# The gate's small working tiles placed in the buffer of the token sums

## Chip, cores, metric

One core of a Trainium2 chip runs the whole program. The metric is the device time of one execution in microseconds (us), smaller being better.

## The reference

Attention with a multiplicative decay, and behind it a mixture of experts in which every expert sees every token and the gate weighs them after eight rounds of normalising over experts and over tokens:

```python
scores = scale * np.matmul(q, k.transpose(0, 1, 3, 2))        # 4 batches, 8 heads, 576 x 64
scores = np.where(causal, -1e9, scores + decay)
attn = softmax(scores); x = (attn @ v) as [2304, 512]

logits = x @ w_gate                                            # 8 experts
P = np.exp(logits - logits.max())
for _ in range(8):
    P /= P.sum(1, keepdims=True) + 1e-09
    P /= P.sum(0, keepdims=True) + 1e-09
    P *= N / E
for e in range(E):
    out += P[:, e:e + 1] * (np.maximum(x @ w1[e], 0.0) @ w2[e])
```

## The kernel before, in words

The attention runs first and leaves x transposed in on-chip memory as two parts, `x_hi` and `x_lo`; every product is made of three matmuls of such parts. Then come the experts. Their work is a list `work` of items (pass n, expert e, quarter fb of the hidden width); a pass takes 768 of the 2304 tokens. In this document "item 0" is the first of that list. Items 0 to 7 alternate experts 1 and 0 and are plain; from item 8 on the first product is the fast form (`first_fast`, seven half-size products, L1032), which needs sums of blocks of x (`T_HI`, `T_LO`) and of w1 (`wsum`).

For each item the program writes, in this order:

- loads of the next item's w1 halves and of this item's w2 halves, all on SP's one queue, in order (L693);
- the first product (`first_plain`, PE L702), with its relu and remainder on ACT (`hh`, L708) and DVE (`hl`, L711);
- the split of the next item's w1 (ACT cast L978, then the remainder on DVE L979; for fast items the sums on POOL, L985 to L999);
- the second product of the item **before** (`second`, PE L722, six 128-token tiles or two, six matmuls each), added into `acc` on DVE;
- the split of this item's w2, in two halves: ACT cast L978, POOL remainder L979. There is one w2 buffer, so these run between one second product and the next. The raw w2 half is free for the next load when L979 has read it.
- in some items, `token_sums(g, c)`: eight POOL operations into the tile `ts` (L958 to L965), an ACT cast of all of it into `T_HI` (L966), and a POOL subtraction for `T_LO` (L967). `ts` has one buffer. In pass 0 they are written after items 3 and 5. A third group, for the next pass, is written later and its POOL operations are brought forward.

The gate's eight rounds (`gate_weights`) are a generator that is advanced a step at a time between matmul groups of items 0 to 4. A round is nine small DVE operations on `prob` and small tiles `rs`, `cs`, `ca`, and one PE matmul with a matrix of ones (`pc`, L941), which waits for DVE's `cs` (L936). The last operation of a round is L945 on DVE.

The order in each engine's queue around this part is made by the recording layer's scheduler: it places an instruction once its inputs and its buffer are there by its own reckoning, so operations may stand well ahead of where the program writes them. At run time each engine goes through its queue in order.

Of the kernel before, what the change touches and what calls it, by code (L numbers as in the profile page):

```python
# [8 lines left out]
F32 = mybir.dt.float32  # L9
# [5 lines left out]
P = 128  # L15
# [117 lines left out]
def attention_then_moe(  # L133
# [14 lines left out]
    E, _, F = w1.shape  # L148
# [6 lines left out]
    NTILE = N // P  # L155
# [707 lines left out]
    HT = N // 6  # L863
# [5 lines left out]
    acc_p = ctx.enter_context(tc.tile_pool(name="acc", bufs=1))  # L869
    tp = ctx.enter_context(tc.tile_pool(name="tp", bufs=1))  # L870
    up = ctx.enter_context(tc.tile_pool(name="up", bufs=1))
    gp = ctx.enter_context(tc.tile_pool(name="gp", bufs=1))
    acc += [acc_p.tile([P, DM], F32, name=f"acc{t}") for t in range(AHEAD // P, PT)]
    acc_1 = [acc_p.tile([P, DM], F32, name=f"acc1_{t}") for t in range(PT)]

# [26 lines left out]

    def gate_weights():

        lg = gp.tile([P, NTILE, E], F32, name="lg")
        pl = psum.tile([P, NTILE, E], F32, tag=GATE, name="pl")

        for a in range(0, N, DM):
            w = min(DM, N - a)
            nc.sync.dma_start(out=acc_1[a // DM][0:E, 0:w], in_=lg_d[:, a:a + w])  # L910
        for _ in range(4):
            yield
        for t in range(NTILE):
            a, o = divmod(t * P, DM)
            nc.tensor.transpose(pl[:, t, :], acc_1[a][0:E, o:o + P], ident[0:E, 0:E])
        nc.vector.tensor_copy(lg, pl)
        mx = gp.tile([P, 1], F32, name="mx")
        nc.vector.tensor_reduce(out=mx, in_=lg.rearrange("p t e -> p (t e)"), axis=AX.X, op=ALU.max)
        yield

        pm = psum.tile([P, P], F32, tag=GATE, name="pm")
        nc.tensor.transpose(pm, mx.to_broadcast([P, P]), ident)
        ma = gp.tile([P, 1], F32, name="ma")
        nc.vector.tensor_reduce(out=ma, in_=pm, axis=AX.X, op=ALU.max)
        nc.vector.tensor_scalar_mul(ma, ma, -1.0)
        nc.scalar.activation(out=prob, in_=lg, func=AF.Exp, bias=ma)
        for _ in range(8):
            rs = gp.tile([P, NTILE], F32, tag="rs", name="rs")
            nc.vector.tensor_reduce(out=rs, in_=prob, axis=AX.X, op=ALU.add)
            nc.vector.tensor_scalar_add(rs, rs, 1.0e-9)  # L930
            nc.vector.reciprocal(rs, rs)
            nc.vector.tensor_tensor(
                out=prob, in0=prob, in1=rs.unsqueeze(2).to_broadcast([P, NTILE, E]), op=ALU.mult
            )
            cs = gp.tile([P, E], F32, tag="cs", name="cs")
            nc.vector.tensor_reduce(out=cs, in_=prob.rearrange("p t e -> p e t"), axis=AX.X, op=ALU.add)  # L936
            for _ in range(3):
                yield
            ca = gp.tile([P, E], F32, tag="ca", name="ca")
            pc = psum.tile([P, E], F32, tag=GATE, name="pc")  # L940
            nc.tensor.matmul(pc, ones, cs, start=True, stop=True)  # L941
            nc.vector.tensor_scalar_add(ca, pc, 1.0e-9)
            nc.vector.reciprocal(ca, ca)
            nc.vector.tensor_scalar_mul(ca, ca, float(N) / E)
            nc.vector.tensor_tensor(  # L945
                out=prob, in0=prob, in1=ca.unsqueeze(1).to_broadcast([P, NTILE, E]), op=ALU.mult
            )
# [166 lines left out]
    for m, (n, e, fb, segs, fast) in enumerate(work):  # L1114
        if m + 1 < len(work):
            r1 = raw("w1", *work[m + 1][1:3])
        r2 = raw("w2", e, fb)
        if m == 0:
            pending.append(gate_weights())
            go_on()  # L1120
        hts = hts_of[m % 2]
        tags = EARLIER if m < PLAIN_0 else FIRST
        if fast:
            first_fast(segs[0][0], hts, tags)
        else:
            first_plain(segs, hts, tags)
        if n > 0 and m in sums_at:
            token_sums(*sums_at[m])
        if m + 1 < len(work):
            if work[m + 1][4]:  # L1130
                split_sums(r1, weight_sums(r1))
            else:
                split_whole("w1", r1, nc.vector)
        if late:
            if late[:3] == (0, 1, GATED):
                while pending:
                    go_on()
            second(*late)
        split_whole("w2", r2, nc.vector if n > 0 and not fast else nc.gpsimd)
        if n == 0 and m in sums_at:  # L1140
            token_sums(*sums_at[m])
        late = (n, e, fb, segs, hts)
# [27 lines left out]
```

## Time and profile before

| | |
|---|---|
| median of 3 runs | 1770.77 us (1770.63 to 1771.16) |
| the profiled execution's own time | 1770.57 us |
| its span, first to last instruction | 1768.8 us |
| granted TensorE clock, mean | 0.996 of full |
| PE busy | 1725.3 us |
| DVE busy | 1344.6 us |
| POOL busy | 1134.9 us |
| ACT busy | 682.8 us |

PE is the tensor engine, PEld its weight loads, DVE the vector, ACT the scalar and POOL the GpSimd engine, SP the one that issues transfers. The time is the span and 1.8 us around it. A busy PE counts a matmul to its modelled end, so what PE loses is read from its waits and from its clock. The gate's rounds lie between 288 and 338 us of the span, and the first fast item begins at 377 us.

### The profile page before, as it was taken

How to read it: one execution, taken by the hardware profiler on the slowest of the kernel's cores; microseconds unless marked ns; L12 is line 12 of the kernel's file. 1: busy time of each engine (PE TensorE's matmuls, PEld its weight loads, DVE VectorE, ACT ScalarE, POOL GpSimd, SP SyncE). 2: the span in 40 equal slices, each digit the busy share in tenths (PEclk: the TensorE clock that was granted, in tenths of full speed). 3: DMA queues.
4: the chain of work that ended last, by engine and by line, in shares of the span. 5: the costliest groups of instructions: out<-in, count | busy, mean ns of one | idle time of the engine just before them, and what ended most of it. 6: DMA issues, size and time to landing. Idle time of an engine off the chain costs nothing.

```text
span 1768.8 us, 26556 instructions
## 1 busy us (share of the span) xinstructions
PE 1725.3 (98%) x9355; PEld 1521.6 (86%) x9355; DVE 1344.6 (76%) x2278; ACT 682.8 (39%) x1456; POOL 1134.9 (64%) x1067
## 2 busy tenths in 40 slices
PE   7999998999999999989999999999999999999998
PEld 5777776788999999879999999999899999999997
DVE  6887785967778777757778777777577877777786
ACT  6766662333333333233333333333333333333332
POOL 6675746366766666666766666676566666667662
PEclk9999999999999999999999999999999999999999
DMA  6433331222222222132212222222311222222221
GB/s 162 127 101 107 104 88 32 90 90 72 61 66 72 72 66 72 54 102 72 64 62 72 72 66 72 72 60 66 107 60 60 72 72 66 72 72 61 65 72 60
DMA packets 146596, 135.20 MB, mean 76 GB/s; under 512 B 65176, under 2 KB 116384, under 8 KB 146464
## 3 DMA queue, kind: packets, MB, share of 16 engines
q1 hardware_dynamic: 146464, 133.52, 24.9%
q8 instruction: 73, 1.20, 0.3%
q14 instruction: 59, 0.48, 0.1%
HBM read 128.61 MB, written 4.87 MB: 75 GB/s over the span
## 4 chain that ended last, share of the span: by engine, by line
PE 73%; POOL 2%; issue 1%; ACT 0%; DVE 0%; DMA 0%; POOLq 0%
PE po L722 39%; PE ph L1032 33%; PE ph L702 1%; POOL t L967 1%; POOL early_w L979 0%; POOL ts L958 0%; ACT t L966 0%; POOL ts L959 0%; DMA w<-in_moe_w_dram 0%; DVE hl L711 0%; POOL ts L964 0%; POOL ts L963 0%; POOL ts L961 0%; POOL ts L965 0%; POOL ts L960 0%
## 5 line engine op out<-in xcount | busy, mean ns | idle before, releaser
L722 PE MATMUL po<-early_w,hh 128*128 128x512 f32 x2304 | 719.7, 393 | 10.9 <-POOL early_w L979 9.2
L722 PEld LDWEIGHTS po<-early_w,hh 128*128 128x128 f32 x2304 | 430.5, 189 | 101.3 <-POOL early_w L979 12.8
L1038 DVE TENSOR_TENSOR u<-ph,u 128x384 f32<-128x384 f32 x588 | 319.9, 556 | 193.9 <-PE ph L1032 188.0
L1083 DVE SCALAR_TENSOR_TENSOR acc<-po,prob,acc 128x512 f32<-128x512 f32 x532 | 381.2, 742 | 102.3 <-PE po L722 102.3
L722 PE MATMUL po<-early_w,hl 128*128 128x512 f32 x1152 | 452.1, 392 | 0.0
L998 POOL TENSOR_TENSOR early_w<-ws,early_w 128x1024 fp32r<-128x1024 f32 x84 | 202.2, 2408 | 280.3 <-ACT early_w L995 280.3
L711 DVE SCALAR_TENSOR_TENSOR hl<-u,hh 128x384 fp32r<-128x384 f32 x336 | 376.6, 1121 | 1.8 <-ACT hh L708 1.7
L978 ACT CAST early_w<-w 128x512 fp32r<-128x512 f32 x216 | 133.7, 622 | 560.7 <-POOL ws L985 442.3
L708 ACT ACTIVATE hh<-u 128x384 fp32r<-128x384 f32 x336 | 175.4, 523 | 297.4 <-DVE u L1038 297.4
L1032 PE MATMUL ph<-t,early_w 128*128 128x384 f32 x1512 | 275.6, 334 | 0.0
L979 POOL TENSOR_TENSOR early_w<-w,early_w 128x512 fp32r<-128x512 f32 x184 | 235.3, 1299 | 59.0 <-ACT early_w L978 59.0
L1032 PEld LDWEIGHTS ph<-t,early_w 128*128 128x128 f32 x1512 | 264.0, 188 | 0.0
L722 PEld LDWEIGHTS po<-early_w,hl 128*128 128x128 f32 x1152 | 217.3, 189 | 45.2
L1032 PE MATMUL ph<-xhi,wa 128*128 128x384 f32 x672 | 199.4, 337 | 0.0
L985 POOL TENSOR_TENSOR ws<-w 128x256 f32<-128x256 f32 x84 | 61.9, 737 | 130.9 <-DMA w<-in_moe_w_dram 130.7
L999 POOL TENSOR_TENSOR wa<-w,wa 128x512 fp32r<-128x512 f32 x84 | 134.1, 1596 | 0.0
L1032 PEld LDWEIGHTS ph<-xhi,wa 128*128 128x128 f32 x672 | 123.8, 188 | 3.3
L1032 PE MATMUL ph<-xlo,wa 128*128 128x384 f32 x336 | 112.9, 336 | 0.0
L702 PE MATMUL ph<-xhi,early_w 128*128 128x384 f32 (+2 forms) x384 | 107.9, 347 | 0.7 <-DVE early_w L979 0.7
L1032 PE MATMUL ph<-t,wa 128*128 128x384 f32 x504 | 100.9, 334 | 0.0
L1032 PE MATMUL ph<-xhi,early_w 128*128 128x384 f32 x336 | 98.7, 334 | 0.0
L987 POOL TENSOR_TENSOR ws<-w 128x256 f32<-128x256 f32 x84 | 86.7, 1032 | 12.0 <-DMA w<-in_moe_w_dram 11.9
(139 smaller groups left out, 2109.1 us busy)
## 6 DMA issues: line engine op xcount, KB each, us to landing
w<-in_moe_w_dram SPq DMA_DIRECT2D x400, 256.0 KB, 2.6
dn<-cum_d SPq DMA_DIRECT2D x16, 576.0 KB, 3.7
out_dram<-acc SPq DMA_DIRECT2D x18, 256.0 KB, 3.6
q<-in_q_dram SPq DMA_DIRECT2D x32, 128.0 KB, 3.2
k<-in_k_dram SPq DMA_DIRECT2D x32, 128.0 KB, 2.7
v<-in_v_dram SPq DMA_DIRECT2D x32, 128.0 KB, 2.3
k<-in_q_dram SPq DMA_DIRECT2D x16, 32.0 KB, 2.4
k<-in_k_dram SPq DMA_DIRECT2D x16, 32.0 KB, 2.1
```

The costliest lines, as they stand in the source:

```text
L702: nc.tensor.matmul(ph[:, 0:w], wt[:, c, fs], xt[:, c, g:g + w], start=(c == 0 and n == 0), stop=(c == KC - 1 and n == 2),)
L708: nc.scalar.activation(out=hh[:, 0:w], in_=ph[:, 0:w], func=AF.Relu)
L711: nc.vector.scalar_tensor_tensor(out=hl[:, 0:w], in0=ph[:, 0:w], scalar=0.0, in1=hh[:, 0:w].bitcast(F32), op0=ALU.max, op1=ALU.subtract)
L722: nc.tensor.matmul(po, ht[:, ts], wt[:, ft, :], start=(ft == 0 and n == 0), stop=(ft == FB - 1 and n == 2))
L978: nc.scalar.copy(out=hi[:, s], in_=r)
L979: lo_on[n % len(lo_on)].tensor_tensor(out=lo[:, s], in0=r, in1=hi[:, s].bitcast(F32), op=ALU.subtract)
L987: tt(out=t[:, 2], in0=a11, in1=a21, op=ALU.subtract)
L998: nc.gpsimd.tensor_tensor(out=wsum[1], in0=t, in1=wsum[0].bitcast(F32), op=ALU.subtract)
L999: nc.gpsimd.tensor_tensor(out=lo[:, 1:3], in0=k1, in1=hi[:, 1:3].bitcast(F32), op=ALU.subtract)
L1032: nc.tensor.matmul(ps, ws[y][:, c], xs[z], start=(c == 0 and n == 0), stop=(c == KH - 1 and n == 2))
L1038: nc.vector.tensor_tensor(out=out, in0=in0, in1=in1, op=ALU.add)
L1083: nc.vector.scalar_tensor_tensor(out=acc[i], in0=po, scalar=prob[:, t, e:e + 1], in1=acc[i], op0=ALU.mult, op1=ALU.add)
```

## The change

The pool `gp` of the gate's small tiles goes. The gate takes one tile of the tag `ts`, the one buffer in which `token_sums` works, and its six small tiles are slices of it. So the buffer is the gate's from its first step to its last.

```diff
-    gp = ctx.enter_context(tc.tile_pool(name="gp", bufs=1))
...
-        lg = gp.tile([P, NTILE, E], F32, name="lg")
+
+        gt = up.tile([P, 4, HT], F32, tag="ts", name="gt")
+        lg = gt[:, 0, 0:NTILE * E].rearrange("p (t e) -> p t e", e=E)
...
-        mx = gp.tile([P, 1], F32, name="mx")
+        mx = gt[:, 1, 0:1]
...
-        ma = gp.tile([P, 1], F32, name="ma")
+        ma = gt[:, 1, 1:2]
...
-            rs = gp.tile([P, NTILE], F32, tag="rs", name="rs")
+            rs = gt[:, 2, 0:NTILE]
...
-            cs = gp.tile([P, E], F32, tag="cs", name="cs")
+            cs = gt[:, 3, 0:E]
...
-            ca = gp.tile([P, E], F32, tag="ca", name="ca")
+            ca = gt[:, 3, E:2 * E]
```

The queues of PE, DVE and SP hold the same work in the same order as before. POOL's and ACT's differ, in one place each. Line numbers from L907 on are one higher in the changed kernel. POOL's queue before, from the last part of x in the attention (`xlo`) on: `ts` and `t` are the token sums, `early_w` is the remainder of w2.

```order
L979 TENSOR_TENSOR early_w_98<-w,early_w_97 128x512 x2
L232 TENSOR_TENSOR xlo<-xf,xhi 128x576 x2
L958 TENSOR_TENSOR ts<-xhi,xlo 128x384
L959 TENSOR_TENSOR ts<-xhi,xlo 128x384
...
L965 TENSOR_TENSOR ts<-ts,xlo 128x384
L967 TENSOR_TENSOR t_4577<-ts,t_4576 128x1536
...
L958 TENSOR_TENSOR ts<-xhi,xlo 128x384
L979 TENSOR_TENSOR early_w_98<-w,early_w_97 128x512
L959 TENSOR_TENSOR ts<-xhi,xlo 128x384
L979 TENSOR_TENSOR early_w_98<-w,early_w_97 128x512
```

Two whole groups of sums stand there, and the third around item 1's two halves of w2. The same place of POOL's queue in the changed kernel, right behind the two `xlo` rows:

```order
L980 TENSOR_TENSOR early_w_98<-w,early_w_97 128x512 x6
L959 TENSOR_TENSOR ts<-xhi,xlo 128x384
...
L966 TENSOR_TENSOR ts<-ts,xlo 128x384
L980 TENSOR_TENSOR early_w_98<-w,early_w_97 128x512
L968 TENSOR_TENSOR t_4574<-ts,t_4573 128x1536
L980 TENSOR_TENSOR early_w_98<-w,early_w_97 128x512
...
L964 TENSOR_TENSOR ts<-ts 128x384
L980 TENSOR_TENSOR early_w_98<-w,early_w_97 128x512
L965 TENSOR_TENSOR ts<-xhi,ts 128x384
L980 TENSOR_TENSOR early_w_98<-w,early_w_97 128x512
L966 TENSOR_TENSOR ts<-ts,xlo 128x384
L988 TENSOR_TENSOR ws<-w 128x256
```

The w2 halves of items 1, 2 and 3 now stand ahead of the first sum. That sum waits for the last round's L946 on DVE (L945 before). Item 4's two halves stand behind the first group and on either side of its `T_LO`. Left out by the third "..." are the second group whole and six operations of the third; behind these come item 5's two halves, then the w1 sum of item 8 (L988).

ACT's queue before, where items 1 and 2 are worked on (`t` is the cast of the sums into `T_HI`):

```order
L708 ACTIVATE hh_4586<-ph 128x256
L966 CAST t_4576<-ts 128x1536
L708 ACTIVATE hh_4590<-ph 128x256
L978 CAST early_w_95<-w 128x512 x2
L926 ACTIVATE prob<-lg,ma 128x144
L966 CAST t_4576<-ts 128x1536
L978 CAST early_w_97<-w 128x512 x2
L708 ACTIVATE hh<-ph 128x384 x2
```

And where the two casts stand in the changed kernel, among the work of items 4 and 5:

```order
L979 CAST early_w_97<-w 128x512
L967 CAST t_4573<-ts 128x1536
L979 CAST early_w_97<-w 128x512
L708 ACTIVATE hh_4583<-ph 128x256
L979 CAST early_w_95<-w 128x512 x2
L708 ACTIVATE hh_4587<-ph 128x256
L967 CAST t_4573<-ts 128x1536
L979 CAST early_w_97<-w 128x512 x2
L708 ACTIVATE hh<-ph 128x384 x2
```

Both casts moved back, the first to between item 4's w2 halves, the second to ahead of item 5's; nothing else moved on ACT.

## Rows read from the trace of the kernel before

**Rows 1.** The page: busy time, share of the span and instructions of each engine.

```profile
PE 1725.3 (98%) x9355; PEld 1521.6 (86%) x9355; DVE 1344.6 (76%) x2278; ACT 682.8 (39%) x1456; POOL 1134.9 (64%) x1067
```

**Rows 2.** PE's waits, 276 to 340 us: total us, times, longest us.

```profile
PE pc L941 <- DVE cs L936: 8.7, 5, 3.9
PE pm L922 <- DVE mx L918: 1.3, 1, 1.3
PE ph L702 <- DVE early_w L979: 0.7, 1, 0.7
```

**Rows 3.** Timeline of ACT: start, length, instruction, [idle before <- releaser].

```profile
285.40 1.48 ACT L966 CAST t<-ts 128x1536 fp32r<-128x1536 f32 x1 [3.88 <-POOL ts L965]
...
299.60 1.47 ACT L966 CAST t<-ts 128x1536 fp32r<-128x1536 f32 x1 [8.10 <-POOL ts L965]
...
302.01 0.48 ACT L708 ACTIVATE hh<-ph 128x384 fp32r<-128x384 f32 x1
```

**Rows 4.** Timeline of DVE behind that activation.

```profile
302.52 0.56 DVE L711 SCALAR_TENSOR_TENSOR hl<-ph,hh 128x384 fp32r<-128x384 f32 x1 [2.80 <-ACT hh L708]
```

**Rows 5.** Timeline of PE: two of the gate's matmuls.

```profile
303.46 0.39 PE L941 MATMUL pc<-cs,ones 128*128 128x8 f32 x2 [3.89 <-DVE cs L936]
...
331.90 0.39 PE L941 MATMUL pc<-cs,ones 128*128 128x8 f32 x2 [1.18 <-DVE cs L936]
```

**Rows 6.** Windows: length, busy PE, PEld, DVE, ACT, POOL (x), clock, DMA, GB/s.

```profile
304.00:308.00 4.00, 4.00 (x16) 4.00 (x15) 3.44 (x10) 0.49 (x1) 3.92 (x4) 0.57 0.00 0
...
345.00:353.00 8.00, 8.00 (x38) 6.66 (x37) 7.86 (x14) 1.18 (x4) 0.16 (x1) 1.00 0.32 102
353.00:361.00 8.00, 8.00 (x48) 8.00 (x47) 3.27 (x6) 2.59 (x6) 2.38 (x2) 1.00 0.20 66
...
759.50:765.00 5.50, 5.48 (x13) 4.32 (x14) 1.50 (x2) 0.92 (x2) 5.27 (x6) 0.50 0.62 196
```

**Rows 7.** DVE lines, 276 to 340 us: duration in ns, least/median/most.

```profile
L932 DVE TENSOR_TENSOR prob<-prob,rs x8: 295/412/1041, 294.1 to 334.5; 128x144 f32<-128x144 f32 x8
L945 DVE TENSOR_TENSOR prob<-prob,ca x8: 299/310/1344, 296.5 to 337.7; 128x144 f32<-128x144 f32 x8
L979 DVE TENSOR_TENSOR early_w<-w,early_w x10: 627/857/1509, 277.5 to 339.5; 128x512 fp32r<-128x512 f32 x10
```

**Rows 8.** Timeline of POOL: the first group of sums, later splits.

```profile
276.36 1.01 POOL L958 TENSOR_TENSOR ts<-xhi,xlo 128x384 f32<-128x384 f32 x1 [4.21 <-DMA lg_d<-lg]
...
284.37 1.00 POOL L965 TENSOR_TENSOR ts<-ts,xlo 128x384 f32<-128x384 f32 x1
286.96 3.47 POOL L967 TENSOR_TENSOR t<-ts,t 128x1536 fp32r<-128x1536 f32 x1 [1.59 <-ACT t L966]
...
341.78 2.73 POOL L979 TENSOR_TENSOR early_w<-w,early_w 128x512 fp32r<-128x512 f32 x2 [10.54 <-ACT early_w L978]
...
363.93 0.88 POOL L987 TENSOR_TENSOR ws<-w 128x256 f32<-128x256 f32 x1 [8.54 <-DMA w<-in_moe_w_dram]
...
366.03 1.18 POOL L997 TENSOR_TENSOR wa<-w,wa 128x256 fp32r<-128x256 f32 x1
```

**Rows 9.** Timeline of DVE: the end of the gate's last round.

```profile
337.73 0.30 DVE L945 TENSOR_TENSOR prob<-prob,ca 128x144 f32<-128x144 f32 x1
```

**Rows 10.** Timeline of PE: fourth and fifth matmul of items 4, 5; fifth of 6.

```profile
345.08 0.63 PE L722 MATMUL po<-early_w,hh 128*128 128x512 f32 x2
...
361.62 0.62 PE L722 MATMUL po<-early_w,hh 128*128 128x512 f32 x2
...
368.49 0.50 PE L722 MATMUL po<-early_w,hh 128*128 128x512 f32 x1 [0.84 <-POOL early_w L979]
```

**Rows 11.** The page: loads of weights, count, KB each, us to landing.

```profile
w<-in_moe_w_dram SPq DMA_DIRECT2D x400, 256.0 KB, 2.6
```

**Rows 12.** Timeline of PE at the second pass's start.

```profile
756.89 0.50 PE L722 MATMUL po<-early_w,hh 128*128 128x512 f32 x1 [3.04 <-POOL early_w L979]
```

## The prediction

> **What bounds the kernel now.** I read the page's busy times first: PE has work for 1725.3 of 1768.8 us [rows 1], no other engine comes near, and what can be won or lost is what PE waits for and where its clock falls. The change lies between 276 and 390 us, so I asked for PE's waits there. Up to 340 us they are seven, 10.7 us together, nearly all on DVE [rows 2]: five times a gate matmul waits for `cs`, 8.7 us, the longest 3.9; once `pm` waits for `mx`, 1.3; once the first product for a w1 remainder, 0.7.
>
> What makes DVE late is seen on ACT [rows 3]. Its queue reaches the cast of the sums, L966, before POOL has made them, and everything behind it stands still: 3.88 us, then 8.10. The `hh` at 302.01 stands behind the second cast; DVE's `hl` waits 2.80 for it [rows 4]; `cs` stands behind `hl` on DVE; and PE's `pc` at 303.46 has waited 3.89 [rows 5]. The first cast in the same way holds an `hh` and `hl` ahead of `mx`, which is the 1.3.
>
> Two more things are paid there. From 304 to 308 us the granted clock is 0.57, and PE makes 16 matmuls in 4.0 us; a stretch of like ones at 1.00 has 48 in 8.0 [rows 6]. So those 16 are worth 2.7, and 1.3 us is lost to the lower of the two levels (1.2 instead of 2.4 GHz), behind a wait of 3.9. And some DVE rows are far longer at times than at others: L932 takes 0.30 to 1.04 us, L945 0.30 to 1.34, the w1 remainder L979 0.63 to 1.51, all of one size each [rows 7]. The long ones are those beside a running POOL; POOL is in the sums from 276 us on [rows 8].
>
> **The change: what it takes away.** No operation is added or dropped; addresses of tiny tiles cost nothing. The sums' first operation must wait for the gate's last, since they share a buffer. So both casts leave their place on ACT, and no sum runs beside the gate. Term by term:
>
> - `pm`: 1.3, all, since its `hh` is free at once.
> - The 3.9 of `pc`: DVE's own chain ends just about when PE gets there, but item 1's w2 remainder on POOL (2.7 for its two halves, [rows 8]) now falls beside it and stretches about two operations by half a us. I take 2.9.
> - The four other `pc` waits sum to 8.7 - 3.9 = 4.8. The one of 1.18 at 331.9 [rows 5] comes after the sums, and stays. Of the 3.6 of the other three I take 3.2, as several stretched rows of 0.5 to 1.0 us each go from their chains [rows 7].
> - The 0.7 for the w1 remainder at 278 us, a stretched L979: all.
> - The lost clock, 1.3.
>
> Sum 1.3 + 2.9 + 3.2 + 0.7 + 1.3 = 9.4 us won. Without any relief of DVE it would be 1.3 + about 2.4 + 1.3 = 5.0; all of it gone would be 10.7 - 1.2 + 1.3 = 10.8. These are the bounds.
>
> **What it costs.** I keep the old clock of the trace here, as everything up to the gate's end moves forward together: PE's last `pc` stands at a fixed place in its queue, and DVE's end of the gate follows it. Prices on POOL [rows 8]: a group of eight sums 9.0 us (276.36 to 285.37), so 1.1 each; then 1.6 until ACT's cast is done and 3.5 for L967; a w2 half 1.3.
>
> - The gate ends at 337.73 + 0.30 = 338.0 [rows 9]. The first group runs 338.1 to 347.1. Item 4's first w2 half follows, to 348.4, inside the 1.6 of the cast. L967 runs 348.7 to 352.2, the second half to 353.5.
> - PE's second product of item 4 needs the first half for its second matmul and the second half for its fifth. That fifth one began at 345.08 + 0.2 = 345.3 [rows 10]; now 353.5. PE waits about 8.
> - POOL goes on with the second group: 353.5 to 362.5, cast, L967 364.1 to 367.6, six sums of the third group to 374.3, item 5's first half to 375.6, one sum, second half to 378.0. PE's fifth matmul for item 5 began at 361.62 + 0.2 = 361.8; now 378.0. PE comes there 16.5 us of own work after 353.5, at 370.0, so it waits another 8, and what POOL does in a row is the bound. The total is 16.2 late. ACT is blocked at its second cast from about 352 to 362.5, and its w2 casts and `hh` behind it are done by 367.5, ahead of POOL; that costs nothing unless POOL's cover goes.
> - Item 6. SP is in order: item 8's w1 load stands behind item 6's second w2 load, which needs the raw half that POOL has read at 378.0. It lands 2.6 us later [rows 11], so L987, behind the eighth sum in POOL's queue, waits until 380.6 (it waited for that load before too, [rows 8]). Then L987 0.9, item 6's first half 1.3, L997 1.2, second half 1.3: 385.3. PE's fifth matmul for item 6, at 368.49 with a wait of 0.84 before [rows 10], is then 16.8 late. PE itself comes there at 378.0 + 368.5 - 0.8 - 361.8 = 383.9 at full clock.
> - The clock. The kernel has the same sight already: at the second pass's start PE waits 3.04 [rows 12] for a half of w2 behind sums, and 759.5 to 765 runs at 0.50 with 13 matmuls, for which 38 in 8.0 us give 2.7 [rows 6]: 2.8 lost. After two waits of 8 I expect it twice. The first time lies under POOL's row and costs nothing. The second brings PE to 386.7, 18.2 late. Between 16.8 and 18.2 I take 17.4, nearer the middle, since the stretch at 304 us lost only 1.3.
>
> Behind item 6 POOL, ACT and PE stand to each other as before, so nothing is won back. The stretch of DVE's rows does not vanish either: from 338 us on four L979 and six scalings of `acc` stand beside the sums, and at the most that rows 7 show, 0.9 each, DVE would be 9 us late [rows 7]. PE stands for 8 in item 4 and 8 in item 5, which covers it; uncovered it would make 17 of the 8 below. The Trainium skill (GPSIMD Engine Reference, 8. Key points) speaks against the move here: GpSimd shares SBUF interfaces with VectorE, and there is contention for instructions with two SBUF inputs or in a two-port mode. By it the stretch only changes its place and the sum is up to 17 without the cover; by the timeline, with POOL as the later one, it stays at 8.
>
> Bounds: sums at 1.05 each and no lost clock, with item 6's old 0.84 taken off, give 13.4; a stretch of low clock more than I count gives 20.
>
> **Sum.** 17.4 - 9.4 = 8.0 us slower. Against the profiled execution's own 1770.57 that is 1778.6 us; the runs' median is 0.2 above that execution.
>
> **Rivals.**
>
> - *The low clock is paid twice, or POOL's row stretches beside DVE*: 20 or a little more lost, 5.0 to 9.4 won, 1781 to 1786 us. For it: two long waits where the trace has single ones of 3 to 4 us. Against: the first falls under POOL's row. 11%.
> - *It balances*: cost at its bound of 13.4 and the gain at 10.8 leave 2.6, 1773.2 us, within 0.2% (3.5 us, about what a measurement of this kernel can tell from no change). For it: with DVE idle behind a standing PE the sums may run at their shortest. Against: the first group runs beside DVE's catching up. 10%.
> - *Faster*: the sums, with neither gate nor busy DVE beside them, run so quickly that POOL reaches item 5's second half before 361.8 + 9.4 = 371.2. That is 33 us for a row that I price at 40, and at its shortest rows still 38. Only then is the wait at item 5 less than what the gate gains; 1769 us at 31 us. Nothing in the trace shows POOL that fast. 5%.
> - *It does nothing*, POOL's sums staying where they were: the order excludes it, since the sums stand behind items 1 to 3 and wait for the gate. In the 10% above.
>
> **How the numbers follow.** The forecast, 4 to 12 us slower, has 74%. With the first rival, slower holds 85%; same 10%; faster 5%. The range is 1773.2, the balanced case, to 1783.5, into the first rival; about one in ten lies below and a little less above.
>
> **What would show it.** In the new profile: no wait of ACT at L967 before 330 us, and hardly a wait of PE at `pc` except that near 332; L959 first starting right after DVE's last L946; two groups of PE waits on POOL's L980 of some 7 to 8 us in items 4 and 5, with the clock near 0.5 behind them; L988 waiting for its load. I am wrong if PE's waits on L980 sum to under 10 us, if PE still waits 3 us or more at a `pc`, or if something behind 400 us has moved.

## The result

The changed kernel takes 1780.4 us (median of 6 runs, 1779.38 to 1781.45), the kernel before, beside it on the same chip, 1770.88 us (1770.63 to 1771.16). The ratio is 1.0051 (95% interval 1.0040 to 1.0062): 9.5 us slower. The profiled execution of the changed kernel took 1781.45 us, its span is 1779.7 us, its mean clock 0.990.

First the page's busy times, which answer [rows 1], then PE's waits from 270 to 420 us (us in total, times, longest), which answer [rows 2] and take in the time behind the gate.

```profile
PE 1731.5 (97%) x9355; PEld 1524.7 (86%) x9355; DVE 1345.4 (76%) x2278; ACT 682.5 (38%) x1456; POOL 1136.9 (64%) x1067
```

```profile
PE po L722 <- POOL early_w L980: 13.0, 4, 4.5
PE pc L942 <- DVE gt L937: 2.7, 3, 1.2
PE po L722 <- DVE acc L1084: 1.2, 2, 1.1
```

The work is the same, and the waits have changed places. At `pc` 2.7 us are left of 8.7; the wait at `pm` and that for the w1 remainder are gone. In their place PE waits 13.0 us for POOL's w2 remainder. That it is POOL's row behind the gate shows in its timeline (start, length, instruction, idle before; L959 to L966 are the eight sums, L968 is `T_LO`, L980 a w2 half):

```profile
328.21 1.27 POOL L959 TENSOR_TENSOR ts<-xhi,xlo 128x384 f32<-128x384 f32 x1 [6.92 <-PE ph L702]
...
336.81 1.05 POOL L966 TENSOR_TENSOR ts<-ts,xlo 128x384 f32<-128x384 f32 x1
337.82 1.45 POOL L980 TENSOR_TENSOR early_w<-w,early_w 128x512 fp32r<-128x512 f32 x1
339.44 3.44 POOL L968 TENSOR_TENSOR t<-ts,t 128x1536 fp32r<-128x1536 f32 x1 [0.17 <-ACT t L967]
342.84 1.71 POOL L980 TENSOR_TENSOR early_w<-w,early_w 128x512 fp32r<-128x512 f32 x1
344.52 1.45 POOL L959 TENSOR_TENSOR ts<-xhi,xlo 128x384 f32<-128x384 f32 x1
...
353.46 1.37 POOL L966 TENSOR_TENSOR ts<-ts,xlo 128x384 f32<-128x384 f32 x1
...
366.86 1.26 POOL L980 TENSOR_TENSOR early_w<-w,early_w 128x512 fp32r<-128x512 f32 x1
...
369.03 1.27 POOL L980 TENSOR_TENSOR early_w<-w,early_w 128x512 fp32r<-128x512 f32 x1
...
373.95 0.73 POOL L988 TENSOR_TENSOR ws<-w 128x256 f32<-128x256 f32 x1 [2.69 <-DMA w<-in_moe_w_dram]
```

The releaser named beside the first sum (PE) is not the real one: the sum starts right behind the gate's last operation on DVE:

```profile
327.78 0.30 DVE L946 TENSOR_TENSOR prob<-prob,gt 128x144 f32<-128x144 f32 x1
```

PE's timeline has the last `pc` that waits, the seventh of the eight rounds, then item 4's and item 5's second products at the two halves of w2:

```profile
321.95 0.39 PE L942 MATMUL pc<-gt,ones 128*128 128x8 f32 x2 [1.19 <-DVE gt L937]
339.32 0.79 PE L722 MATMUL po<-early_w,hh 128*128 128x512 f32 x1 [4.25 <-POOL early_w L980]
344.61 0.79 PE L722 MATMUL po<-early_w,hh 128*128 128x512 f32 x1 [3.64 <-POOL early_w L980]
368.17 0.79 PE L722 MATMUL po<-early_w,hh 128*128 128x512 f32 x1 [4.53 <-POOL early_w L980]
370.35 0.80 PE L722 MATMUL po<-early_w,hh 128*128 128x512 f32 x1 [0.54 <-POOL early_w L980]
```

Windows answer to [rows 6]: length, busy PE, PEld, DVE, ACT, POOL (instructions), clock, DMA, GB/s.

```profile
304.00:308.00 4.00, 4.00 (x28) 3.67 (x27) 3.90 (x11) 1.63 (x3) 2.18 (x2) 1.00 0.41 131
340.00:345.00 5.00, 1.36 (x4) 0.64 (x3) 4.72 (x3) 1.48 (x4) 5.00 (x3) 0.50 0.18 52
345.00:350.00 5.00, 5.00 (x13) 3.84 (x13) 3.52 (x6) 0.00 (x0) 4.92 (x5) 0.50 0.48 157
370.00:375.00 5.00, 4.65 (x15) 3.88 (x16) 2.29 (x4) 1.72 (x4) 2.31 (x4) 0.53 0.48 163
```

The low clock at 304 us is gone (28 matmuls in 4 us, not 16), and two such stretches stand behind the two long waits.

To place gain and cost I set each kernel's start of the first fast item (PE's first matmul of L1032, after the change L1033) against its own last `xlo` on POOL, ahead of everything that changes. The two rows in the kernel before, then in the changed one:

```profile
270.74 1.41 POOL L232 TENSOR_TENSOR xlo<-xf,xhi 128x576 fp32r<-128x576 f32 x1 [10.06 <-DVE xhi L224]
377.28 0.33 PE L1032 MATMUL ph<-xhi,wa 128*128 128x384 f32 x1
```

```profile
271.13 1.41 POOL L232 TENSOR_TENSOR xlo<-xf,xhi 128x576 fp32r<-128x576 f32 x1 [10.06 <-DVE xhi L224]
387.15 0.33 PE L1033 MATMUL ph<-xhi,wa 128*128 128x384 f32 x1
```

Before, that is 377.28 - 270.74 = 106.5 us; after, 387.15 - 271.13 = 116.0 us, 9.5 later. PE's seventh `pc` moved from 331.90 to 321.95 (and the eighth and last, 336.42 before, by as much), while the `xlo` row moved 0.4 the other way: 10.3 us won at the gate, so 19.8 lost behind it.

### The profile page after: what moved, and what is told of

Read it like the earlier page. It is cut to its first block, busy times and chain, and to the rows that moved or that the text cites. A ratio compares the mean times of both kernels' runs of the same rounds, so it can differ in the third digit from the quotient of the medians.

```text
span 1779.7 us, 26554 instructions
## 1 busy us (share of the span) xinstructions
PE 1731.5 (97%) x9355; PEld 1524.7 (86%) x9355; DVE 1345.4 (76%) x2278; ACT 682.5 (38%) x1456; POOL 1136.9 (64%) x1067
## 4 chain that ended last, share of the span: by engine, by line
PE 73%; POOL 2%; issue 1%; ACT 0%; DVE 0%; DMA 0%; POOLq 0%
PE po L722 39%; PE ph L1033 33%; PE ph L702 1%; POOL t L968 1%; POOL early_w L980 0%; POOL ts L959 0%; ACT t L967 0%; POOL ts L960 0%; DMA w<-in_moe_w_dram 0%; DVE hl L711 0%; POOL ts L964 0%; POOL ts L962 0%; POOL ts L965 0%; POOL ts L966 0%; POOL ts L961 0%
## 5 line engine op out<-in xcount | busy, mean ns | idle before, releaser
L980 POOL TENSOR_TENSOR early_w<-w,early_w 128x512 fp32r<-128x512 f32 x184 | 235.7, 1301 | 71.7 <-ACT early_w L979 71.7
L1033 PE MATMUL ph<-t,early_w 128*128 128x384 f32 x1512 | 275.6, 334 | 0.0
L1033 PEld LDWEIGHTS ph<-t,early_w 128*128 128x128 f32 x1512 | 264.0, 188 | 0.0
L1033 PE MATMUL ph<-xhi,wa 128*128 128x384 f32 x672 | 199.4, 337 | 0.0
L986 POOL TENSOR_TENSOR ws<-w 128x256 f32<-128x256 f32 x84 | 62.0, 738 | 130.5 <-DMA w<-in_moe_w_dram 130.4
L1033 PEld LDWEIGHTS ph<-xhi,wa 128*128 128x128 f32 x672 | 123.8, 188 | 3.3
L1033 PE MATMUL ph<-xlo,wa 128*128 128x384 f32 x336 | 112.9, 336 | 0.0
L1033 PE MATMUL ph<-t,wa 128*128 128x384 f32 x504 | 100.9, 334 | 0.0
L1033 PE MATMUL ph<-xhi,early_w 128*128 128x384 f32 x336 | 98.7, 334 | 0.0
L996 ACT CAST early_w<-ws 128x1024 fp32r<-128x1024 f32 x84 | 87.0, 1035 | 10.3 <-POOL ws L989 7.4
```

Source lines behind the costliest of these rows:

```text
L980: lo_on[n % len(lo_on)].tensor_tensor(out=lo[:, s], in0=r, in1=hi[:, s].bitcast(F32), op=ALU.subtract)
L996: nc.scalar.copy(out=wsum[0], in_=t)
L1033: nc.tensor.matmul(ps, ws[y][:, c], xs[z], start=(c == 0 and n == 0), stop=(c == KH - 1 and n == 2))
```

## The experiments

In all runs the kernel before ran on the same chip (1771.6 us in the first four, 1772.0 in the next four, 1771.6 in the last two). The second column is the first fast item's start against the kernel before, measured as above; the third the span against the 1768.8 us of before, less that item's own shift, so what comes behind it. Both are read from one profiled execution of each kernel, which lies up to 1.2 us off the median beside it.

| kernel | first fast item, us | behind it, us | median, us | ratio to before (95%) |
|---|---|---|---|---|
| changed | +9.5 | +1.0 | 1780.4 | 1.0051 (1.0040 to 1.0062) |
| buffer held only | +9.3 | +0.1 | 1780.72 | 1.0048 (1.0036 to 1.0061) |
| sums left out | -9.5 | +5.5 | 1766.66 | 0.9973 (0.9962 to 0.9983) |
| third group held | +2.2 | +5.0 | 1778.53 | 1.0038 (1.0025 to 1.0052) |
| and item 4 on DVE | +0.7 | +5.8 | 1777.46 | 1.0034 (1.0022 to 1.0047) |
| casts on POOL | +0.7 | +0.6 | 1771.59 | 1.0000 (0.9991 to 1.0009) |
| and `T_LO` in four | +2.0 | +1.3 | 1775.65 | 1.0020 (1.0011 to 1.0029) |
| changed, sums on DVE | -11.1 | -9.2 | 1750.5 | 0.9878 (0.9863 to 0.9893) |
| before, sums on DVE | -10.1 | -13.8 | 1746.91 | 0.9860 (0.9846 to 0.9873) |
| before, later sums on DVE | +4.3 | -13.9 | 1761.49 | 0.9943 (0.9929 to 0.9956) |
| changed, later sums on DVE | +8.3 | -13.8 | 1765.4 | 0.9964 (0.9951 to 0.9976) |

**The buffer held, the tiles left.** The gate keeps its pool `gp`, and a tile of the tag `ts` is held beside it:

```diff
         lg = gp.tile([P, NTILE, E], F32, name="lg")
+        gt = up.tile([P, 4, HT], F32, tag="ts", name="gt")
...
+        nc.vector.tensor_copy(gt[:, 0, 0:1], lg[:, 0, 0:1])
...
+        nc.vector.tensor_copy(gt[:, 0, 0:1], prob[:, 0, 0:1])
```

> The kernel before, with the gate's small tiles left in their own pool; only the buffer of the token sums is held for the length of the gate by a tile of its own, with one tiny DVE copy into it at the gate's start and one at its end. No operand of the gate has moved. If the whole effect is the wait for the buffer: the time of the changed kernel within 1.5 us, 1779 to 1782, and POOL's order that of the changed kernel. If where the small tiles lie matters too: off by more than that.

1780.72 us, as the changed kernel, with POOL's queue in the changed kernel's order and PE's waits on POOL at the same four places (4.26, 3.63, 5.66 and 0.54 us). Within what these runs can tell (8.7 us slower here, 9.5 there), the whole effect is the wait for the buffer; where the small tiles lie costs nothing that can be measured.

**The sums left out.** The first pass's sums are not computed, and the third group is held back as in the next kernel:

```diff
     def token_sums(g, c):
+        if g == 0:
+            for x in (T_HI, T_LO):
+                nc.gpsimd.tensor_copy(x[:, c].rearrange("p a t -> p (a t)"), zero.to_broadcast([P, 4 * HT]))
+            return
...
+    HOLD = 9
...
+        if m == HOLD:
+            held = up.tile([P, 4, HT], F32, tag="ts", name="held")
+            nc.scalar.copy(out=held[:, 0, 0:1], in_=hts[0][0][0][:, 0:1].bitcast(F32))
```

> As the kernel with the third group held back, but the first pass's token sums are left out: T_HI and T_LO of that pass are filled with zeros by four operations on POOL (so its output is not the reference's). What is left is the gain alone: gate beside a free POOL and a free ACT, and nothing behind it. My theory (9.4 us to be won beside the gate, 10.3 as read from the trace of the changed kernel): 9 to 11 us faster than before, 1760 to 1762. Rival (the gain is partly lent: what PE gains at the gate is taken back behind it by DVE, which has its operations with acc still to do): 5 to 8 us faster, 1763 to 1766, with PE waits on DVE in items 4 to 6.

At the first fast item it is 9.5 us ahead, what I expected of the gate; in the end only 5.0 us. So the time fits the rival, but not by the rival's cause: from 340 to 400 us PE waits 1.3 us on DVE (1.1 before). The loss is that of the third group, which is held until item 9 here and then stands in POOL's row: from 400 to 430 us PE waits 3.2 us on POOL, as in the next run.

**The third group held back**, by the last four added lines above alone, on the changed kernel.

> The changed kernel, with the buffer of the token sums taken once more for a moment, at the end of item 9, so that the third group of sums (for the next pass) can no longer be brought forward into items 5 and 6. POOL then goes from the second group's T_LO straight to item 5's two w2 halves. My theory (the cost is the row of work on POOL behind the gate, item by item, and each operation taken from the row gives its time back): the eight sums of the third group are 8 to 9 us on POOL, so item 5's second wait falls from about 8 to about 0 to 1 and item 6's load comes earlier by as much; 9 to 11 us faster than the changed kernel, 1769 to 1772, that is level with before. Rival (the cost is the low clock behind the long waits and DVE's stretched rows, which one wait of 8 us is enough to bring): under 5 us faster than the changed kernel, 1776 or more.

Item 5's wait goes as expected: PE does not wait there, and the first fast item begins 7.3 us earlier than in the changed kernel. But the median is only about 2 us better: the rival's number, for another reason than the rival's. The group has found no free place; it comes back at item 10. POOL's timeline there, then PE's waits from 400 to 430 us:

```profile
404.92 1.01 POOL L959 TENSOR_TENSOR ts<-xhi,xlo 128x384 f32<-128x384 f32 x1
...
412.79 1.33 POOL L966 TENSOR_TENSOR ts<-ts,xlo 128x384 f32<-128x384 f32 x1
```

```profile
PE po L722 <- POOL early_w L980: 3.2, 2, 3.0
```

Between the second product's start at 413.85 and the next first product's at 427.49 it loses 5.4 us on the kernel before: the wait and what follows from it. My expectation had the first half of this right, and missed that an operation taken from one full row of POOL must go into another.

**Item 4's w2 remainder on DVE as well.**

```diff
-        split_whole("w2", r2, nc.vector if n > 0 and not fast else nc.gpsimd)
+        split_whole("w2", r2, nc.vector if n > 0 and not fast or m == 4 else nc.gpsimd)
```

> The kernel with the third group held back, and beside it both w2 remainders of item 4 made on DVE instead of POOL, so that neither of the two groups of sums left behind the gate stands ahead of a w2 half that PE is about to need. My theory: the 8 us wait of item 4 goes too, the gain beside the gate stays: 7 to 10 us faster than before, 1761 to 1764. Rival (DVE is itself late behind the gate, with its rows stretched beside the sums, so that item 4's halves come late from DVE too): PE waits 3 to 8 us on DVE in item 4 instead, 1765 to 1770.

1777.46 us: neither my range nor the rival's. In item 4 PE's wait changes its cause and stays. Rows of PE, ACT, DVE and POOL:

```profile
340.34 0.79 PE L722 MATMUL po<-early_w,hh 128*128 128x512 f32 x1 [3.29 <-ACT early_w L979]
343.88 0.80 PE L722 MATMUL po<-early_w,hh 128*128 128x512 f32 x1 [2.75 <-DVE early_w L980]
```

```profile
338.29 1.47 ACT L967 CAST t<-ts 128x1536 fp32r<-128x1536 f32 x1 [6.42 <-POOL ts L966]
339.67 0.61 ACT L979 CAST early_w<-w 128x512 fp32r<-128x512 f32 x1
```

```profile
340.37 3.46 DVE L980 TENSOR_TENSOR early_w<-w,early_w 128x512 fp32r<-128x512 f32 x1 [1.83 <-issue]
```

```profile
339.84 3.44 POOL L968 TENSOR_TENSOR t<-ts,t 128x1536 fp32r<-128x1536 f32 x1 [1.58 <-ACT t L967]
```

ACT's cast of the sums is again in its queue ahead of a cast that PE needs, and stands 6.42 us for POOL. Then DVE's remainder, which elsewhere takes 0.69 us, takes 3.46: it starts while POOL's `T_LO` runs (339.84 to 343.28) and ends 0.55 us after it, at 343.83. What that says of DVE's long rows stands in the last section.

**ACT freed, DVE not.** On the kernel before, the casts go to POOL:

```diff
-        nc.scalar.copy(out=T_HI[:, c], in_=t)
+        if g:
+            nc.scalar.copy(out=T_HI[:, c], in_=t)
+        else:
+            nc.gpsimd.tensor_copy(T_HI[:, c], t)
```

> The kernel before, with one operation moved to another engine: the casts of the token sums into T_HI in the first pass are made on POOL instead of ACT, each at the end of its group of sums. The sums themselves stay beside the gate, where they were. So ACT no longer stands still 3.9 and 8.1 us for them, but DVE's operations still run beside a busy POOL. My theory (most of what the change wins comes from the two blocked stretches of ACT, the long pc wait and the pm wait with the clock lost behind them, about 5 of the 9.4 us; the stretch of DVE's rows is worth the rest): 4 to 6 us faster than before, 1765 to 1767 us; PE's wait at pm gone, no pc wait over 2 us. Rival (the gain is DVE's relief from POOL, and ACT's standstill costs next to nothing): 0 to 2 us faster, 1769 to 1771, with the pc waits still summing to 7 or more.

Nothing is won: my theory falls, and the rival's size holds (pc waits 8.4 in all, in 4). The waits of 3.88 and 8.10 on ACT [rows 3] are gone, and so is `pm`'s. What takes their place is seen on DVE, on POOL and at PE:

```profile
287.98 2.83 DVE L982 TENSOR_TENSOR early_w<-w,early_w 128x512 fp32r<-128x512 f32 x1
...
301.52 2.95 DVE L944 TENSOR_SCALAR ca<-ca 128x8 f32<-128x8 f32 x1
```

```profile
286.75 3.50 POOL L970 TENSOR_TENSOR t<-ts,t 128x1536 fp32r<-128x1536 f32 x1
...
300.95 3.50 POOL L970 TENSOR_TENSOR t<-ts,t 128x1536 fp32r<-128x1536 f32 x1
```

```profile
307.29 0.60 PE L941 MATMUL pc<-cs,ones 128*128 128x8 f32 x2 [3.16 <-DVE cs L936]
```

A DVE operation on 8 columns, 0.17 us at other times, takes 2.95 and ends at 304.47, when POOL's operation ends (304.45). The w1 remainder of 287.98 ends at 290.81, 0.56 behind POOL's 290.25. In the kernel before, with ACT's cast in the way, DVE came to the same two operations nearer the end of POOL's, and they took 1.51 and 0.28 us. So ACT's standstill had kept DVE from standing there for POOL.

**The same, `T_LO` in four pieces.**

```diff
-        tt(out=T_LO[:, c], in0=t, in1=T_HI[:, c].bitcast(F32), op=ALU.subtract)
+        for n in range(4):
+            tt(out=T_LO[:, c, n], in0=t[:, n], in1=T_HI[:, c, n].bitcast(F32), op=ALU.subtract)
```

> The kernel before with the casts of the sums on POOL, as in the first experiment, and POOL's subtraction for T_LO (one operation of 128x1536, 3.5 us) cut into four of 128x384, of the same work in all. My theory, formed on the trace of the first experiment: a DVE operation on two inputs in on-chip memory (or its tensor_scalar there) that meets a running POOL operation stands until that one operation ends, and then takes its own time. So the length of a single POOL operation decides: the 2.83 us w1 remainder and the 2.95 us tensor_scalar of 128x8 of the first experiment fall to at most 1.7 and 1.3, the pc waits behind them (2.5 and 3.2) to about 1 each, and the kernel is 2 to 4 us faster than the first experiment, 1767 to 1769. Rival (the two engines share the bandwidth, so that only the total of POOL's work counts): no change, 1771 to 1772, with stretched rows of the same sum.

DVE's rows do as the theory says: no 2.83 and 2.95 any more, the longest from 287 to 308 us is 1.44, and the `pc` waits fall from 8.4 to 5.4 us, none above 1.2. Yet the kernel is 3.7 us slower than with one piece (each against the kernel before beside it), not 2 to 4 faster. The four pieces take 4.85 and 3.97 us where the one took 3.50, and now PE waits for POOL itself, at item 1's w2 remainder, which stands behind two groups in POOL's queue:

```profile
287.86 4.85 POOL L971 TENSOR_TENSOR t<-ts,t 128x384 fp32r<-128x384 f32 x4
...
302.95 3.97 POOL L971 TENSOR_TENSOR t<-ts,t 128x384 fp32r<-128x384 f32 x4
```

```profile
311.36 0.50 PE L722 MATMUL po<-early_w,hh 128*128 128x512 f32 x1 [4.26 <-POOL early_w L983]
```

So three limits lie close together beside the gate: ACT behind the casts, DVE behind POOL's long operations, and POOL's own row. Before, item 1's second product began at 310.29 and POOL's first half for it was done at 307.06, the second at 309.34; with the casts on POOL and `T_LO` in four it begins at 306.71 and stands for POOL; in the changed kernel it begins at 302.79. Taking the sums away from there, as the change does, lifts all three at once.

**The sums on DVE**, in the changed kernel and in the kernel before:

```diff
-        tt = nc.gpsimd.tensor_tensor
+        tt = nc.vector.tensor_tensor
```

> The changed kernel with all token sums made on DVE instead of POOL (the ACT casts stay), so that POOL does nothing but its splits and sums of w1. The gate still holds the buffer, so the sums stand behind it, on DVE. By DVE's rows (0.6 us for 128x512 from two inputs in on-chip memory with POOL quiet) a group is about 4 us and T_LO 1.8, where POOL needed 9 to 10 and 3.5. My theory (the cost is POOL's row behind the gate and POOL's hold on DVE): the 9.4 us won beside the gate stay, DVE is 3 to 6 us late in items 4 and 5, and the waits on POOL's sums at the two later pass starts (about 3 us and a low clock each) go or shrink: 4 to 9 us faster than before, 1763 to 1767. Rival (DVE, which has scalings of acc to do there, becomes the bound behind the gate): 8 us or more of PE waits on DVE in items 4 to 6, 1769 to 1774.

> The kernel before with all token sums made on DVE instead of POOL: the sums lie between the gate's operations on DVE, as its queue has them, and no POOL operation runs beside the gate but the w2 remainders. My theory (POOL's hold on DVE cost the gate 5 to 9 us): two groups put about 11 us of DVE work between the gate's operations of some 50 us, in which DVE was idle or standing for about 18; the pc waits change their cause more than their sum, 6 to 10 us; behind the gate nothing is late; the pass starts gain as in the kernel beside it: 1765 to 1770. Rival (work of DVE's own in the chain is worse than standing for POOL): pc waits over 12 us, 1773 or more.

Both are far faster than I expected, 21.5 and 25.1 us below the kernel before: these versions beat both kernels, and the better one is without the hold. The busy times of that one, and its PE waits from 270 us to the end:

```profile
PE 1718.4 (98%) x9355; PEld 1519.5 (87%) x9355; DVE 1361.0 (78%) x2332; ACT 683.8 (39%) x1456; POOL 1066.8 (61%) x1013
```

```profile
PE pc L941 <- DVE cs L936: 3.0, 4, 1.0
PE po L722 <- POOL early_w L979: 1.7, 3, 1.1
PE po L722 <- DVE acc L1083: 1.2, 2, 1.1
```

The `pc` waits fall to 3.0 us, where I had put them at 6 to 10, though DVE makes 16 us of sums among the gate's operations from 276 to 330 us. The scheduler puts more PE work between the `pc` there (341 matmuls from the last `xlo` to the last `pc`, where the kernel before has 272): the last begins at 339.93, not 336.42, and behind it, up to 400 us, PE waits about 2 us in both. In the hold's version the first fast item is 1.0 earlier still, but DVE is then over 97% busy from 330 to 390 us, POOL's work on w1 gets late, and PE waits 2.3 us for it and 1.5 on DVE: behind the first fast item it gains 4.6 us less. With sums on DVE the change costs 3.6 us.

**Which of that is the gate's.** The last two kernels make only the later passes' sums on DVE:

```diff
-        tt = nc.gpsimd.tensor_tensor
+        tt = nc.vector.tensor_tensor if g else nc.gpsimd.tensor_tensor
```

> The kernel before with the first pass's two groups of sums on POOL as they were, and only the groups of the two later passes on DVE. In the runs with all sums on DVE the first fast item began 8.7 (no hold) and 10.6 us (hold) earlier than before, and the rest of the 20 to 25 us came behind it, where before has PE waits of 4.7 and 3.0 us on POOL at the pass starts with a low clock behind each. My theory (these later gains have nothing to do with the gate): the first fast item begins within 2 us of before's, and the kernel is 12 to 16 us faster, 1756 to 1760. Rival (the third group, which POOL makes beside the gate, is part of what the gate suffers from): the first fast item 4 us or more earlier, 1754 or less.

> The changed kernel with the first pass's two groups on POOL, held behind the gate as the change has it, and the later groups on DVE, so that the third group neither stands in POOL's row behind the gate nor is put off to item 10. My theory (the third group cost 6.8 of the change's 19.3 behind the gate, as the held kernel showed, and nothing takes its place here): the first fast item begins 2 to 4 us later than before's, the change costs 2 to 5 us against the kernel beside it (its like without the hold), 1759 to 1764. Rival (the third group on DVE falls into items 5 and 6, where DVE holds POOL up): 7 us or more against the kernel beside it, 1765 or more.

Behind the first fast item both win 13.8 to 13.9 us, as the kernel before with all sums on DVE does. That part belongs to the pass starts: matmul by matmul against the kernel before, the first of the two kernels gains 8.3 us at the second pass's start, 5.5 at the third's and nothing between. There the kernel before waits on POOL, with the low clock behind [rows 6, 12], and neither of these two waits. The kernel before, PE's waits from 740 to 780 and from 1240 to 1290 us:

```profile
PE po L722 <- POOL early_w L979: 4.7, 2, 3.0
```

```profile
PE po L722 <- POOL early_w L979: 3.0, 1, 3.0
```

Ahead of the first fast item they came 2 and 4 us later than I had allowed, and both medians lie about 1.5 us above my ranges; the second is in the rival's range by its time, but not by its 7 us against the kernel beside it. The third group now waits on DVE for the buffer that POOL's second group holds, and DVE's queue stands still with it, in the first kernel in the middle of the gate:

```profile
304.84 1.61 DVE L958 TENSOR_TENSOR ts<-xhi,xlo 128x384 f32<-128x384 f32 x1 [9.26 <-POOL t L967]
```

```profile
312.09 0.59 PE L941 MATMUL pc<-cs,ones 128*128 128x8 f32 x2 [10.23 <-DVE cs L936]
```

The change costs 3.9 us between these two, but each pays for such a standstill (7.5 us in the second), so this pair doesn't price the third group. The held kernel does.

## Why the prediction was right, point by point

**What it takes away.** 9.4 was forecast; the trace after gives 10.3, and the kernel without sums 9.5. Set matmul by matmul against the kernel before, the terms came out one by one: the w1 remainder 0.8 (forecast 0.7), `pm` 1.6 (1.3), the long `pc` 3.0 (2.9; a wait of 0.9 is left), the other three 3.4 (3.2), the lost clock 1.5 (1.3). The `pc` wait of 1.18 at 331.9 stayed, as said. But the terms don't stand side by side as I added them. The lower bound, 5.0 with no relief of DVE, was not reached when it was tried: with ACT free and DVE still beside the sums nothing was won. So the 1.3 of `pm`, the 2.4 of `pc` and the 1.3 of the clock, which I put down to ACT alone, could be won only with the sums gone too. What I missed there is POOL's own row as the next limit, and I took DVE's long rows for a stretch of at most 0.9 us, where the length of POOL's operation sets it.

**What it costs.** 17.4 was forecast, 19.8 measured, by the steps named: two sets of waits in items 4 and 5, `L988` waiting for its load, low clock behind both waits. The step that was mis-sized is POOL's row. I priced it at 39.9 us from the first sum to the end of item 5's second half; it took 42.1 (328.21 to 370.30). The first group took 9.65 and the second 10.3 in place of 9.0, item 4's halves 1.45 and 1.71 in place of 1.3. So item 5's fifth matmul is 18.5 late (370.35 - 0.4 - 361.8 + 10.3), not 16.2; from there to the first fast item 1.3 is lost, where I had 1.2.

The trace shows why the row was longer: POOL stands for DVE, as DVE does for POOL. Of the 23 sums in this row, 14 are longer than 1.02 us. Each of the 14 starts while a DVE operation runs that reads none of PE's banks (a w1 remainder, or a scaling of `acc`), and ends 0.85 to 0.88 us behind the end of that operation. Item 4's two halves end 1.12 behind one. An example of DVE and of POOL in the changed kernel; DVE ends at 330.02, POOL at 330.90:

```profile
328.51 1.51 DVE L980 TENSOR_TENSOR early_w<-w,early_w 128x512 fp32r<-128x512 f32 x1
```

```profile
329.44 1.46 POOL L960 TENSOR_TENSOR ts<-xhi,xlo 128x384 f32<-128x384 f32 x1
```

Two more details differ. PE's wait in item 5 is 5.1 us and not 8, since PE needed 3.2 us more than forecast to come there from item 4, with the low clock behind item 4's wait (0.52 from 344.6 to 351 us). That lies under POOL's row and changes nothing, as the prediction says. And the cover held: behind the gate PE waits 1.2 us on DVE, before 1.3.

**The sum.** 19.8 - 10.3 = 9.5 against a forecast 8.0; both terms came out larger, and their errors partly cancel. By the third group held back, 7.3 of the 19.8 is that group, and the other two 12.5. The bound of 13.4 on the cost comes out nearer 13.7 when its own terms are added again; nothing turned on it.

**The rivals.** Half of the first rival came: POOL's row did stretch beside DVE, and 19.8 is near its 20; but the gain was 10.3, above the 5.0 to 9.4 that it allowed, and so the time stayed under 1781. "Faster" needed a row of 33 us, and it took 42. That something behind 400 us moved, which I named as a sign of error, is true of the profiled execution by about 1 us: at the third pass's start its clock is 0.72 from 1277 to 1281 us, where before it is 1.00 at the same work. The six runs of the changed kernel spread over 2.1 us, those of before over 0.5; whether this stretch is the reason was not tested. The kernel that only holds the buffer, of the same effect, loses only 0.1 us behind its first fast item, so nothing shows the 1 us to be the change's.

**The page.** The prediction weighed the contention between GpSimd and VectorE as a stretch. The Trainium skill (SBUF — State Buffer, Who interferes with whom) says more: the shared port pair is an exclusive lock. The rows here agree: DVE operations of 0.17 and 0.69 us took 2.95 and 3.46, and ended 0.02 and 0.55 us behind POOL's operation.

## What to carry to other kernels

Where several engines' queues meet in one stretch, a wait that is read off one of them is worth only what the next limit leaves: ask of each wait which engine would be late next, POOL's row among them. An operation that is pushed out of a busy stretch has to be priced where it lands, with everything that stands behind it in that queue, and a buffer shared across engines stops a whole in-order queue. When sums on POOL stand in the way of both PE and DVE, try them on DVE: here, at about 0.55 against 1.0 us for most of them, they cost less even where DVE is the engine waited for.

## What the hardware showed that I had not expected

Of DVE's operations between 276 and 340 us in the kernel before, 15 are longer than their like by a quarter of a us or more. Each starts while a POOL operation runs and ends just behind that one operation: the five w1 remainders 0.55 us later (their own time is 0.63), the five multiplications of `prob` 0.15 to 0.17, the five tensor_scalar operations on 8 or 18 columns 0.03 to 0.04. By these rows it is no sharing of bandwidth: DVE stands until POOL's operation is over, be it 1.0 or 3.5 us long. It holds in the other direction too, as the long sums of the changed kernel show. Reciprocals (0.19 to 0.27), reductions (0.28 to 0.44) and operations that read PE's banks (`hl` 0.49 to 0.56 at 384 columns, the copies into `acc` 0.67 to 0.68) keep their time beside the same POOL operations.

And cutting a POOL operation in four, to let DVE in earlier, made it dearer: 3.97 us for 3.50 where POOL hardly stood for DVE, and 4.85 where two of the pieces, 1.48 each, began while a w1 remainder on DVE was running.
